# Attention and MLP in one kernel: products with values in three uneven blocks a pair of heads, and four other pieces of work issued later

## The chip, the cores and the metric

The kernel runs on one core of a Trainium2 chip. The metric is the device time of one execution in microseconds (us); lower is better. The engines are named as in the profile: PE is TensorE (matrix products), PEld its loading of weights, DVE VectorE, ACT ScalarE, POOL GpSimd, and SP SyncE, which here issues every DMA.

## The reference, cut to what matters

```python
xn = layernorm(x)                                   # x: 2048 x 640
q, k, v = split(xn @ wqkv)                          # 32 heads of 20
scores = where(0 <= i - j < 256, q @ k.T * 20**-0.5, -1e9)
s = (softmax(scores) @ v) @ wo
h = relu(xn @ w1 + b1) ** 2                         # 1536 wide
g = silu(h @ w2 + b2)
return x + s * g
```

All inputs are float32. A row of scores sees itself and 255 rows before it, so a tile of 128 rows needs three tiles of keys.

## The kernel before, in words

**Precision.** Every product of projections and of the MLP is made three times, from a high part (rounded by an ACT copy) and a low part (the rest, a subtraction on DVE or POOL) of each operand: high x high, high x low, low x high. Weights come as raw tiles by DMA (`piece`, three raw buffers), ACT makes the high part, and `subtract` (line 758) puts the low parts off: each is queued with `later(0.9 + 0.7 * k, go)` (line 771).

**First stage, to about 116 us.** x is normalized, transposed and split; the values v, and the first group of q and k are made and stored to DRAM; the normalized x goes to DRAM too (`xs_d`).

**The scan, to about 775 us.** It goes over 16 pairs of heads with 16 steps each. Step s makes the scores of one tile of queries for both heads (`scores`, tile sps), whose row maxima DVE takes (`maxima`; `max_rows` transposes four steps' maxima at a time, and small DMAs put them beside q as extra rows, `qs<-mrow`). Nine steps later (LAG) the transposed scores of one tile of keys are made (`scores_t`, tile stps, one buffer), ACT takes the exponential into a tile p (`exps`, eight buffers), and POOL masks two corners. Another two steps later (PLAG, line 45) the tile p is due for the products with the values. These are made in blocks: at each fourth step `values(p, g)` (line 533) multiplies the four tiles p of steps 4g to 4g + 3 into one PSUM bank `ot` of four columns of 128 queries. A head's values are only 21 wide (20 and a column of ones, which gives the sum of the row), so a product uses a strip of 32 columns of PE, and four strips work side by side. Then `evac` copies two finished columns to SBUF (`osb`) with ACT and stores them to `o_d[g]`, one DRAM tensor for each quarter of the queries.

**Fillers.** Between these products the planner puts the other products of the kernel (the remaining groups of q and k, then the MLP). They run in two halves of 64 rows that work side by side. The order of all instructions is written out by this Python code as it runs: a clock of its own (`clock`) advances by a price for each product (`COST`, line 42, and PV = 1.57 for a block of values), `pace` (line 1199) is the price of everything divided by the steps, and `fill(upto)` (line 1201) takes filler products until the clock has reached a time. In each step the scores come first, then fillers to 0.4 of the step (line 1257), then, where due, the block of values, else fillers to the step's end (lines 1262 to 1266). `later(wait, fn)` issues something when this clock has gone on by `wait`.

**DMAs.** All go through SP in the written order. Large loads wait in `bulk`, and `issue` (line 683), called twice a step with 0.9, starts them against a credit: each has a price (`load_xb`, line 853: ten loads of 256 KB of the normalized x at 0.4 each; loads of q and k at 0.7).

**The MLP** goes over eight blocks (two halves of its width, each over four blocks of 512 rows): first products into `hps` (relu and square), then into `yps` in eight groups (four row tiles by two halves of 320 columns), whose sums `ysb` DVE adds to b2 or to the first half's (`yin`, loaded from DRAM).

**The end.** When a quarter of the queries has all its pairs, `invert` (line 1055) loads its row sums, takes the reciprocal on DVE and stores it. `load(u)` (line 1098) loads an eighth of the attention's result with these reciprocals, `turn_out` multiplies and splits it, and the output stage (`out_filler`, from about 783 us) multiplies it with wo, with g and adds x. In the last block of the MLP `late()` (line 913) calls the first such loads at the start of its fourth and fifth group of products.

Of the kernel before, what the change touches and what calls it, by code (L numbers as in the profile page):

```python
# [15 lines left out]
P = 128  # L16
# [5 lines left out]
NT = S // P  # L22
# [18 lines left out]
WARM2 = 10  # L41
COST = {P: 0.067, 2 * P: 0.12, HALF: 0.147, 3 * P: 0.172, BT: 0.23}
SCALE = DH ** -0.5
PV = 1.57
PLAG = 2
NEG = -1.0e30
EPS = 1e-5
SETTLE = 0.45
# [5 lines left out]
def f32(ap):  # L54
    return ap.bitcast(F32)
# [3 lines left out]
def attn_mlp_kernel(ctx: ExitStack, tc, x, wqkv, wo, w1, b1, w2, b2, out):  # L59
# [470 lines left out]

    ot = po_.tile([P, 4, P], F32, tag="o", name="ops")

    def values(p, g):
        for kb in range(4 * g, 4 * g + 4):
            pt = pts.pop((p, kb))
            ts = range(kb, min(kb + 3, NT))
            same, other = [t for t in ts if t % 2 == kb % 2], [t for t in ts if t % 2 != kb % 2]
            parts = [same] if kb % 8 < 6 else [[t] for t in same]
            for part in parts + [other]:
                for hh in range(2):  # L540
                    if not part:
                        continue
                    t = part[0]
                    r0 = 32 * (2 * hh + t % 2)
                    c0 = t // 2 % 4
                    first = t % 8 < 2 and kb == max(0, t - 2) or kb == 0
                    nc.tensor.matmul(ot[r0:r0 + VW, c0:c0 + len(part), :], vps[p][:, kb // 4, kb % 4, hh, :], pt[:, hh, :].rearrange("p (t n) -> p t n", n=P)[:, t - kb:part[-1] - kb + 1:2, :], start=first, stop=part[0] == kb, skip_group_check=True)  # L547
        clock[:2] = [max(clock[:2]) + PV] * 2

        def evac():  # L550
            osb = at2.tile([P, 2, P], F32, tag="osb", name="osb")
            nc.scalar.activation(osb, ot[:, 2 * g % 4:2 * g % 4 + 2, :], AF.Copy)
            post(o_d[g][p], osb.rearrange("p e n -> p (e n)"), 0.8)
        later(SOON, evac)


# [201 lines left out]
    def subtract(tag, jobs):  # L758
        left = [len(jobs)]

        def put_off(k, job):
            def go():
                if item in lows:
                    lows.remove(item)
                    job()
                    left[0] -= 1
                    if not left[0]:
                        held[0] -= 1
            item = (tag, go)
            lows.append(item)  # L770
            later(0.9 + 0.7 * k, go)
        for k, job in enumerate(jobs):
            put_off(k, job)

# [78 lines left out]
    def load_xb(b):  # L853
        xb = [bigp.tile([P, KC * BT], F32R, tag="big", name=f"xb{p}_{b}") for p in range(2)]
        cs = [slice(c * BT, (c + 1) * BT) for c in range(KC)]
        its = [bulk_dma(0.4, f32(xb[p])[:, c], xs_d[p][b][:, c]) for p in range(2) for c in cs]
        return xb, its

    def filler():
# [53 lines left out]
        def late():  # L913
            j = lates[0]
            lates[0] += 1
            if j >= 3:
                load(0)
            if j >= 4:
                load(1)
            if j >= 6:  # L920
                turn_out(0, 0)
            if j >= 7:
                turn_out(0, 1)
                load(2)

        for n, (hf, b) in enumerate(blocks):
# [13 lines left out]
            def used(n=n, b=b, nxt=nxt):  # L940
                if n == NB - 1:
                    shut.discard("11")
                if n == last:
                    shut.discard("o")
                if n < last and blocks[n + 1][1] != b:
                    nxt.extend(load_xb(blocks[n + 1][1]))
            parts = [(th, fp) for th in range(2) for fp in range(WIDE // 2, NFH // 2)]
            parts[len(parts) // 2:len(parts) // 2] = range(WIDE)
            for m, u in enumerate(parts):
# [95 lines left out]
        return 4 * (u // 2) + u % 2 + 2 * t2  # L1045

    def stored(g):
        return NP * NT - NT + 4 * g + 3 + LAG + PLAG

    rec_d = [dram.tile([2, H, MT], F32, name=f"rec_{g}") for g in range(NB)]  # L1050
    recs = {}

    lates = [0]

    def invert():
        for g in range(NB):
            over = state[2] >= 10 ** 6
            if not over and state[2] < stored(g) + 3:
                return
            if g not in recs:  # L1060
                rows = o_d[g].rearrange("p (h r) n -> (p h) r n", h=2)
                recs[g] = at2.tile([P, P], F32, tag="rec", name="rec")
                for par in range(2):
                    nc.sync.dma_start(recs[g][64 * par:64 * (par + 1)], rows[:, 32 * par + DH].rearrange("h (j n) -> h j n", n=P))
            elif recs[g] is not None and (state[2] >= stored(g) + 5 if not over else True):
                nc.vector.reciprocal(recs[g], recs[g])
                nc.sync.dma_start(rec_d[g].rearrange("a h (j n) -> (a h j) n", n=P), recs[g])
                recs[g] = None

    def room_of(tag, name):  # L1070
        if tag == "p32":
# [124 lines left out]

    fl = filler()
    steps = NP * NT + LAG + PLAG
    pace = (8 * (KC - 1) * 15 * COST[BT] + 2 * NB * (15 * (WIDE * COST[BT] + 2 * (NFH - WIDE) * COST[MT]) + 8 * 18 * COST[HALF]) + NP * (2 * NT * COST[3 * P] + NB * PV)) / (steps - 1)

    def fill(upto):
        soon()
# [10 lines left out]
    with tc.manual_schedule(engines={E_.PE, E_.Activation, E_.DVE, E_.Pool, E_.SP}):  # L1213
# [7 lines left out]
        for s in range(steps):  # L1221
            state[2] = s
            vload[0] = 0.2 * (s % 4 == 0) + 0.5 * (s % 4 == 3)
            post_all()
            invert()
            if s >= NP * NT - NT + LAG + 2:
                fetch_y()
            issue(RATE)
            a, b, e = (at_step(s - lag) for lag in (0, LAG, LAG + PLAG))
            if a:  # L1230
                p, q = a
                if q == 0:
                    ensure_bulk(loads)
                if s == 2:
                    ones_rows(1)
                if q == 2 and p < NP - 1:
                    assert made_for(p + 1, 0)
                    loads = [bulk_dma(0.7, *l) for l in pair_loads(p + 1, 0)]
                if q == LAG and p < NP - 1:
                    assert made_for(p + 1, 1)  # L1240
                    loads += [bulk_dma(0.7, *l) for l in pair_loads(p + 1, 1)]
                if q == LAG + 4 and p < NP - 1:
                    load_v(p + 1)
            rows = None
            if a:
                sc = scores(p, q)
            if b:
                stp = scores_t(*b)
            if s % 4 == 0 and 0 < s <= NP * NT:
                rows = max_rows((s - 1) // NT, (s - 1) % NT // 4, stp[0] if b else pair_tile())  # L1250
            if a:
                maxima(*a, *sc)
            if b:
                exps(*b, *stp)
            if rows:
                rows()
            fill((s + EARLY_FILL) * pace)
            post_all()
            issue(RATE)
            flush()  # L1260
            tick()
            if e and e[1] % 4 == 3:
                fill((s + 1) * pace - PV)
                values(e[0], e[1] // 4)
            else:
                fill((s + 1) * pace)
        finish()
# [30 lines left out]
```

## Time and profile before

| | us |
|---|---|
| median of three runs | 859.34 (858.82 to 859.89) |
| the profiled execution's own time | 859.53 |
| its span, first to last instruction | 857.8 |
| last block of values starts | 774.7 |
| first output product starts | 782.9 |

The profile is that of one execution. Busy time is summed by engine; a row of a group has the line, the engine, the operation, output and inputs, how often it ran, busy time and the mean of one, and the idle time of the engine before it. A row of the timeline has the start, the time to the end of the group of like instructions (counted with x), the engine and the line, and in brackets how long the engine stood idle before, and for whom. In the table by windows each engine's busy time stands with its number of instructions, then PE's clock (1.00 is full speed), the DMA share and GB/s. A row of waits has the total, the number and the longest.

### The profile page before, as it was taken

To read this page: it belongs to the slowest core of one execution; us is meant where nothing else is said; L and a number is where in the kernel's file an instruction comes from. 1 tells how busy PE (TensorE), PEld (TensorE's weight loads), DVE (VectorE), ACT (ScalarE), POOL (GpSimd) and SP (SyncE) were. 2 spreads that over 40 slices of the span, in tenths; PEclk is the share of its full clock that TensorE was granted. 3 is DMA by queue.
4 is the path that set the end of the run, shared out by engine and by line. 5 is a ranking of instruction groups with operands and counts; after the bars stand their busy time and mean duration, and the time that the engine had idled before them with its cause. 6 is when DMAs were issued, how large, how long until landed. Compare 5 with 4: busy or idle time off the path is not lost.

```text
span 857.8 us, 25542 instructions
## 1 busy us (share of the span) xinstructions
PE 845.3 (99%) x10160; PEld 786.1 (92%) x10160; DVE 459.1 (54%) x1370; ACT 421.6 (49%) x792; POOL 328.7 (38%) x652
## 2 busy tenths in 40 slices
PE   9999999999999999999999999999999989999998
PEld 8999999888888899999999989999999989999997
DVE  7652136656577545455445466655445444435764
ACT  5222114545556753754654764854754743753321
POOL 6010002334333553553543543643543533541443
PEclk9999999999999999999999999999999999999999
DMA  7997587869889564355266245585376274367992
GB/s 250 327 399 279 170 206 267 263 210 286 278 260 275 146 215 130 84 172 151 77 198 184 61 130 162 144 256 165 77 208 191 61 229 127 126 155 198 277 258 111
DMA packets 94366, 166.42 MB, mean 194 GB/s; under 512 B 10920, under 2 KB 43816, under 8 KB 93224
## 3 DMA queue, kind: packets, MB, share of 16 engines
q1 hardware_dynamic: 94248, 164.80, 63.3%
q8 instruction: 80, 1.31, 0.6%
q14 instruction: 38, 0.31, 0.1%
HBM read 93.66 MB, written 70.52 MB: 191 GB/s over the span
## 4 chain that ended last, share of the span: by engine, by line
PE 93%; DMA 2%; DVE 2%; ACT 1%; issue 1%; SPq 1%; POOL 0%; DVEq 0%
PE hps L469 20%; PE yps L469 20%; PE qkps L469 13%; PE ops L547 10%; PE wops L607 8%; PE vps L229 8%; PE stps L519 5%; PE sps L479 4%; PE qkps L206 3%; PE tps L173 1%; DMA qs<-mrow 1%; DMA qs<-q_d 1%; DMA yin<-y 1%; DVE junk L487 0%; DMA xt<-in_A_x_dram 0%
## 5 line engine op out<-in xcount | busy, mean ns | idle before, releaser
L487 DVE CUSTOM_DVE_ANT_0 junk<-sps,mask 128x384 bf16<-128x384 f32 (+2 forms) x512 | 272.6, 532 | 251.7 <-PE hps L469 70.1
L525 ACT ACTIVATE p<-stps 128x768 f32<-128x768 f32 (+2 forms) x256 | 197.5, 772 | 264.6 <-PE stps L519 216.2
L526 POOL TENSOR_SCALAR_AFFINE_SELECT p<-p 128x256 f32<-128x256 f32 x256 | 107.7, 421 | 332.7 <-ACT p L525 327.8
L469 PE MATMUL yps<-w,hh 64*128 64x320 f32 x1536 | 229.2, 311 | 1.8 <-DVE ysb L996 1.7
L469 PE MATMUL hps<-xb,w 64*128 64x256 f32 (+1 forms) x2100 | 218.6, 305 | 0.0
L469 PEld LDWEIGHTS hps<-xb,w 64*128 64x128 f32 x2100 | 199.2, 187 | 6.2 <-issue 5.1
L469 PEld LDWEIGHTS yps<-w,hh 64*128 64x128 f32 x1536 | 182.2, 186 | 7.5 <-issue 3.4
L469 PE MATMUL yps<-w,hl 64*128 64x320 f32 x768 | 173.5, 310 | 0.0
L479 PE MATMUL sps<-ks,qs 60*128 60x384 f32 (+2 forms) x512 | 141.5, 341 | 1.3 <-DVE mt L487 1.1
L519 PE MATMUL stps<-qs,ks 62*128 62x384 f32 (+2 forms) x512 | 134.5, 332 | 2.4 <-DMA qs<-mrow 2.4
L469 PEld LDWEIGHTS yps<-w,hl 64*128 64x128 f32 x768 | 113.5, 186 | 1.8 <-issue 1.7
L469 PE MATMUL qkps<-xT,wgkh 64*128 64x512 f32 x320 | 100.6, 395 | 0.0
L469 PE MATMUL qkps<-xT,wgqh 64*128 64x512 f32 x320 | 98.1, 392 | 0.0
L528 POOL TENSOR_SCALAR_AFFINE_SELECT p<-p 128x256 f32<-128x256 f32 x224 | 94.1, 420 | 0.0
L547 PE MATMUL ops<-p,vp 128*21 128x128 f32 (+1 forms) x2112 | 92.8, 313 | 0.0
L519 PEld LDWEIGHTS stps<-qs,ks 62*128 62x128 f32 x512 | 87.1, 188 | 3.4 <-issue 2.7
L479 PEld LDWEIGHTS sps<-ks,qs 60*128 60x128 f32 x512 | 85.3, 185 | 4.2 <-DVE mt L487 2.7
L547 PEld LDWEIGHTS ops<-p,vp 128*21 128x21 f32 x2112 | 65.2, 100 | 23.6 <-issue 11.4
L229 PE MATMUL vps<-wv,xT 128*128 128x320 f32 x480 | 71.5, 308 | 0.0
L229 PEld LDWEIGHTS vps<-wv,xT 128*128 128x128 f32 x480 | 70.5, 188 | 0.1
L966 POOL TENSOR_TENSOR hl<-sq,hh 128x512 fp32r<-128x512 f32 x48 | 62.2, 1296 | 19.0 <-ACT sq L965 18.8
L607 PE MATMUL wops<-wo,oT 128*128 128x320 f32 x384 | 61.6, 309 | 0.7 <-DVE ysb L996 0.7
(104 smaller groups left out, 1166.8 us busy)
## 6 DMA issues: line engine op xcount, KB each, us to landing
ks<-k_d SPq DMA_DIRECT2D x64, 240.0 KB
qs<-q_d SPq DMA_DIRECT2D x64, 240.0 KB
xb<-xs SPq DMA_DIRECT2D x60, 256.0 KB
xs<-xT SPq DMA_DIRECT2D x8, 1280.0 KB
k_d<-shm SPq DMA_DIRECT2D x19, 512.0 KB
q_d<-shm SPq DMA_DIRECT2D x19, 512.0 KB
y<-ysb SPq DMA_DIRECT2D x28, 320.0 KB
o<-osb SPq DMA_DIRECT2D x64, 128.0 KB
```

Source lines behind the costliest of these rows:

```text
L206: nc.tensor.matmul(ps, wt[:, c, :], xT[part][b][:, c * BT + t0:c * BT + t0 + n], start=m == 1, stop=m == 3 * KC)
L229: nc.tensor.matmul(ps, xT[xp][b][:, c * BT + t * P: c * BT + (t + 1) * P], wv[wp][:, c, nh * HALF:(nh + 1) * HALF], start=first and m == 0 ...
L469: return nc.tensor.matmul(out, a[r], b_[r], skip_group_check=True, **kw)
L479: nc.tensor.matmul(ss[hh][:, :nk], qs[i][o, q * P:(q + 1) * P], ks[i][o, k0 * P:k0 * P + nk], start=True, stop=True)
L487: nc.vector.tensor_tensor_reduce(out=junk[:, :nk], in0=ss[hh][:, :nk], in1=mask[:, 3 * P - nk:], scale=1.0, scalar=-3.0e38, op0=ALU.add, o ...
L519: nc.tensor.matmul(tps[:, hh, :n], ks[i][o, kb * P:(kb + 1) * P], qs[i][o, kb * P:kb * P + n], start=True, stop=True)
L525: nc.scalar.activation(p32[:, :, :n], tps[:, :, :n], AF.Exp, scale=SCALE)
L526: nc.gpsimd.affine_select(p32[:, :, 0:P], p32[:, :, 0:P], pattern=[[0, 2], [1, P]], compare_op=ALU.is_ge, fill=0.0, base=0, channel_multip ...
L528: nc.gpsimd.affine_select(p32[:, :, 2 * P:], p32[:, :, 2 * P:], pattern=[[0, 2], [-1, P]], compare_op=ALU.is_gt, fill=0.0, base=0, channel ...
L547: nc.tensor.matmul(ot[r0:r0 + VW, c0:c0 + len(part), :], vps[p][:, kb // 4, kb % 4, hh, :], pt[:, hh, :].rearrange("p (t n) -> p t n", n=P ...
L607: nc.tensor.matmul(ps, a, b_, start=j == 0, stop=j == n - 1)
L966: nc.gpsimd.tensor_sub(hh[1][:, :BT], sq, f32(hh[0]))
```

## The change

Five edits go together. The products with values of a pair of heads come in three blocks, of steps 0 to 5, 6 to 11 and 12 to 15 (`CUTS`), in place of four of four steps, each with its own price for the planner (`PVS`), and they are due one step after the exponential in place of two (`PLAG`). The copy of a block's result is of three columns, in one or two instructions, and its stores are cut where the quarter changes; they are posted without the wait of 0.8. Low parts of weights are put off by 1.0 more. Loads of x are issued 1.0 later and at a price of 0.6. In the MLP's last block the first load of the attention's result moves from the fourth group to the fifth. The inversions follow the new blocks: each quarter is stored at another step, is loaded two steps (in place of three) after that and inverted at four (in place of five), only one may be under way at a time, with one buffer, and after the scan a count of calls keeps a load and its inversion apart.

```diff
--- before.py
+++ after.py
@@ -41,8 +41,9 @@
 WARM2 = 10
 COST = {P: 0.067, 2 * P: 0.12, HALF: 0.147, 3 * P: 0.172, BT: 0.23}
 SCALE = DH ** -0.5
-PV = 1.57
-PLAG = 2
+CUTS = (0, 6, 12, NT)
+PVS = (2.25, 2.25, 1.42)
+PLAG = 1
 NEG = -1.0e30
 EPS = 1e-5
 SETTLE = 0.45
@@ -530,8 +531,9 @@
 
     ot = po_.tile([P, 4, P], F32, tag="o", name="ops")
 
-    def values(p, g):
-        for kb in range(4 * g, 4 * g + 4):
+    def values(p, i):
+        lo, hi = CUTS[i], CUTS[i + 1]
+        for kb in range(lo, hi):
             pt = pts.pop((p, kb))
             ts = range(kb, min(kb + 3, NT))
             same, other = [t for t in ts if t % 2 == kb % 2], [t for t in ts if t % 2 != kb % 2]
@@ -545,12 +547,19 @@
                     c0 = t // 2 % 4
                     first = t % 8 < 2 and kb == max(0, t - 2) or kb == 0
                     nc.tensor.matmul(ot[r0:r0 + VW, c0:c0 + len(part), :], vps[p][:, kb // 4, kb % 4, hh, :], pt[:, hh, :].rearrange("p (t n) -> p t n", n=P)[:, t - kb:part[-1] - kb + 1:2, :], start=first, stop=part[0] == kb, skip_group_check=True)
-        clock[:2] = [max(clock[:2]) + PV] * 2
+        clock[:2] = [max(clock[:2]) + PVS[i]] * 2
 
         def evac():
-            osb = at2.tile([P, 2, P], F32, tag="osb", name="osb")
-            nc.scalar.activation(osb, ot[:, 2 * g % 4:2 * g % 4 + 2, :], AF.Copy)
-            post(o_d[g][p], osb.rearrange("p e n -> p (e n)"), 0.8)
+            c0, c1 = lo // 2, hi // 2
+            osb = at2.tile([P, 3, P], F32, tag="osb", name="osb")
+            c = c0
+            while c < c1:
+                n = min(4 - c % 4, c1 - c)
+                nc.scalar.activation(osb[:, c - c0:c - c0 + n], ot[:, c % 4:c % 4 + n, :], AF.Copy)
+                c += n
+            for g in range(c0 // 2, (c1 + 1) // 2):
+                d0, d1 = max(c0, 2 * g), min(c1, 2 * g + 2)
+                post(o_d[g][p, :, (d0 - 2 * g) * P:(d1 - 2 * g) * P], osb[:, d0 - c0:d1 - c0].rearrange("p e n -> p (e n)"))
         later(SOON, evac)
 
 
@@ -768,7 +777,7 @@
                         held[0] -= 1
             item = (tag, go)
             lows.append(item)
-            later(0.9 + 0.7 * k, go)
+            later(1.9 + 0.7 * k, go)
         for k, job in enumerate(jobs):
             put_off(k, job)
 
@@ -853,7 +862,7 @@
     def load_xb(b):
         xb = [bigp.tile([P, KC * BT], F32R, tag="big", name=f"xb{p}_{b}") for p in range(2)]
         cs = [slice(c * BT, (c + 1) * BT) for c in range(KC)]
-        its = [bulk_dma(0.4, f32(xb[p])[:, c], xs_d[p][b][:, c]) for p in range(2) for c in cs]
+        its = [bulk_dma(0.6, f32(xb[p])[:, c], xs_d[p][b][:, c]) for p in range(2) for c in cs]
         return xb, its
 
     def filler():
@@ -913,9 +922,8 @@
         def late():
             j = lates[0]
             lates[0] += 1
-            if j >= 3:
+            if j >= 4:
                 load(0)
-            if j >= 4:
                 load(1)
             if j >= 6:
                 turn_out(0, 0)
@@ -943,7 +951,7 @@
                 if n == last:
                     shut.discard("o")
                 if n < last and blocks[n + 1][1] != b:
-                    nxt.extend(load_xb(blocks[n + 1][1]))
+                    later(1.0, lambda: nxt.extend(load_xb(blocks[n + 1][1])))
             parts = [(th, fp) for th in range(2) for fp in range(WIDE // 2, NFH // 2)]
             parts[len(parts) // 2:len(parts) // 2] = range(WIDE)
             for m, u in enumerate(parts):
@@ -1045,27 +1053,35 @@
         return 4 * (u // 2) + u % 2 + 2 * t2
 
     def stored(g):
-        return NP * NT - NT + 4 * g + 3 + LAG + PLAG
+        return NP * NT - NT + min(c for c in CUTS if c >= 4 * (g + 1)) - 1 + LAG + PLAG
 
     rec_d = [dram.tile([2, H, MT], F32, name=f"rec_{g}") for g in range(NB)]
     recs = {}
 
     lates = [0]
+    calls, ready = [0], [0]
 
     def invert():
+        calls[0] += state[2] >= 10 ** 6
         for g in range(NB):
             over = state[2] >= 10 ** 6
-            if not over and state[2] < stored(g) + 3:
+            if over and calls[0] < ready[0]:
+                return
+            if not over and state[2] < stored(g) + 2 or over and calls[0] < ready[0]:
                 return
             if g not in recs:
+                if any(r is not None for r in recs.values()):
+                    return
+                ready[0] = calls[0] + 3
                 rows = o_d[g].rearrange("p (h r) n -> (p h) r n", h=2)
-                recs[g] = at2.tile([P, P], F32, tag="rec", name="rec")
+                recs[g] = at2.tile([P, P], F32, tag="rec", bufs=1, name="rec")
                 for par in range(2):
                     nc.sync.dma_start(recs[g][64 * par:64 * (par + 1)], rows[:, 32 * par + DH].rearrange("h (j n) -> h j n", n=P))
-            elif recs[g] is not None and (state[2] >= stored(g) + 5 if not over else True):
+            elif recs[g] is not None and (state[2] >= stored(g) + 4 if not over else True):
                 nc.vector.reciprocal(recs[g], recs[g])
                 nc.sync.dma_start(rec_d[g].rearrange("a h (j n) -> (a h j) n", n=P), recs[g])
                 recs[g] = None
+                ready[0] = calls[0] + 2
 
     def room_of(tag, name):
         if tag == "p32":
@@ -1196,7 +1212,7 @@
 
     fl = filler()
     steps = NP * NT + LAG + PLAG
-    pace = (8 * (KC - 1) * 15 * COST[BT] + 2 * NB * (15 * (WIDE * COST[BT] + 2 * (NFH - WIDE) * COST[MT]) + 8 * 18 * COST[HALF]) + NP * (2 * NT * COST[3 * P] + NB * PV)) / (steps - 1)
+    pace = (8 * (KC - 1) * 15 * COST[BT] + 2 * NB * (15 * (WIDE * COST[BT] + 2 * (NFH - WIDE) * COST[MT]) + 8 * 18 * COST[HALF]) + NP * (2 * NT * COST[3 * P] + sum(PVS))) / (steps - 1)
 
     def fill(upto):
         soon()
@@ -1259,9 +1275,10 @@
             issue(RATE)
             flush()
             tick()
-            if e and e[1] % 4 == 3:
-                fill((s + 1) * pace - PV)
-                values(e[0], e[1] // 4)
+            if e and e[1] + 1 in CUTS:
+                i = CUTS.index(e[1] + 1) - 1
+                fill((s + 1) * pace - PVS[i])
+                values(e[0], i)
             else:
                 fill((s + 1) * pace)
         finish()
```

## The prediction, made before the changed kernel was run

> **What bounds the kernel now.** I read the page's busy shares first, then the table by stage, then the chain of waits, and last the timeline around single blocks and stalls.
>
> ```profile
> span 857.8 us, 25542 instructions
> PE 845.3 (99%) x10160; PEld 786.1 (92%) x10160; DVE 459.1 (54%) x1370; ACT 421.6 (49%) x792; POOL 328.7 (38%) x652
> PE 93%; DMA 2%; DVE 2%; ACT 1%; issue 1%; SPq 1%; POOL 0%; DVEq 0%
> 524.00:746.00 222.00, 219.52 (x3169) 204.59 (x3165) 114.35 (x396) 125.09 (x240) 102.20 (x211) 0.99 0.55 158
> 782.80:857.80 75.00, 70.63 (x480) 70.40 (x480) 46.35 (x64) 19.13 (x28) 31.09 (x30) 0.99 0.74 212
> ```
>
> PE is busy 99% of the span, and the last stage (output products, from 782.8) runs almost without a gap until 853.5. In the long stage shown (524 to 746) PE lacks 2.5 us in 222, and one stall makes nearly all of that. So only two things can move the time: what PE's own work costs, switches between kinds of products included, and a handful of stalls. DVE at 54% and ACT at 49% do not bound as averages, but they decide when a score bank comes free.
>
> **The blocks of values, fixed cost.** One pair of heads has 66 products with values, seen as 132 records. They run in four column strips; all others around them run in two halves of 64 rows.
>
> ```profile
> L547 PE MATMUL ops<-p,vp 128*21 128x128 f32 x1344 | 88.6, 274 | 0.0
> L547 PE MATMUL ops<-p,vp 128*21 128x256 f32 x768 | 75.1, 382 | 0.0
> 161.30:171.70 10.40, 1.52 (x40) 1.14 (x40) 0.00 (x0) 0.38 (x1) 1.00 0.90 266
> 180.90:190.50 9.60, 1.28 (x28) 0.90 (x28) 0.00 (x0) 0.38 (x1) 1.00 0.67 211
> ```
>
> 128 more columns cost 382 - 274 = 108 ns a record, 0.216 us a product of two records. In a strip the longest queue of the block of steps 12 to 15 is five such units, 1.08 us; of steps 4 to 7 six, 1.30 us. The table by windows shows 1.28 and 1.52 busy, so about 0.21 us of a block does not depend on its length.
>
> ```profile
> 319.43 0.45 PE L469 MATMUL yps<-w,hh 64*128 64x320 f32 x3
> 319.81 1.52 PE L547 MATMUL ops<-p,vp 128*21 128x256 f32 x40
> 321.25 0.41 PE L469 MATMUL yps<-w,hl 64*128 64x320 f32 x1
> 321.26 0.44 PE L479 MATMUL sps<-ks,qs 60*128 60x384 f32 x1
> 321.51 0.31 PE L469 MATMUL yps<-w,hh 64*128 64x320 f32 x1
> 321.54 0.34 PE L519 MATMUL stps<-qs,ks 62*128 62x384 f32 x1
> ```
>
> Three costs belong to one block. Ahead of it: the last of the three yps products (0.31 each) starts at 319.57, the block at 319.81; of these 0.24 us the product needs the 0.147 that line 42 books for it, so 0.09 are lost. Inside: the block begins at 319.81 and the next product at 321.25, 1.44 us for 1.30 of columns, 0.14 lost. Behind it: the two restarting products take 0.41 and 0.44 where their like take 0.31 and 0.34, 0.10 lost. Sum 0.33 us a block. The change makes 3 blocks of 4 in each of 16 pairs, with the same products: 16 x 0.33 = **5.3 us less**. Bounds: 16 x 0.14 = 2.2 if only the part inside goes, and 16 x 0.36 = 5.8 by the planner's own prices (4 x 1.57 = 6.28 against 2.25 + 2.25 + 1.42 = 5.92). I take 5.3, the sum of what the rows show.
>
> [...]
>
> **The blocks of values, what becomes late.** A step is booked at 638.7/266 = 2.40 us (line 1199), after the change at 632.9/265 = 2.39. Fillers run to 0.4 of it, 0.96, then comes the block. Booked at 2.25 it ends at 3.21, 0.82 into the next step, which so has 1.57 us left until the next pair of scores; before, 0.96 + 1.57 = 2.53 left 2.27. After a block of four steps (1.42) nothing is short. So in 32 of the 256 steps the engines that empty the banks have about 1.6 us.
>
> ```profile
> 301.90 0.34 PE L519 MATMUL stps<-qs,ks 62*128 62x384 f32 x1
> 303.74 0.41 POOL L528 TENSOR_SCALAR_AFFINE_SELECT p<-p 128x256 f32<-128x256 f32 x1
> 303.98 0.33 PE L479 MATMUL sps<-ks,qs 60*128 60x384 f32 x1
> 304.15 0.33 PE L519 MATMUL stps<-qs,ks 62*128 62x384 f32 x1
> 305.55 0.25 ACT L500 ACTIVATE row<-stps 8x128 f32<-8x128 f32 x1
> 306.49 0.33 PE L479 MATMUL sps<-ks,qs 60*128 60x384 f32 x1
> 306.72 0.34 PE L479 MATMUL sps<-ks,qs 60*128 60x384 f32 x1
> 308.14 0.08 DVE L487 DVE_READ_ACCUMULATOR2_ANT mt<- 128x1 f32 x1
> L888 DVE TENSOR_TENSOR slo<-qkps,shm 128x512 fp32r<-128x512 f32 x32 | 22.0, 687 | 6.6 <-ACT shm L885 6.6
> ```
>
> DVE's second maximum is out at 308.22, 1.73 us after the step's first score product (306.49); the second score product of the next step, which reuses that bank, comes 0.23 after its first. With 1.6 us between steps it is asked for at 1.83: 0.10 to spare where DVE has nothing else, and a wait of 0.4 to 0.6 where a subtraction (0.69 in the row of slo, the low parts some less) stands ahead. The first block ends so in step 6 of a pair; the second (steps 6 to 11) ends in the next pair's row 0, whose maxima are only 128 wide. There the bank of stps decides: its row of maxima is read until 305.80, 1.65 after 304.15, a wait of about 0.05. Behind a waiting score product the whole of PE queues, and POOL, ACT and DVE with it. I take 0.06 us on average over 32 steps, **2.0 us more**; bounds nothing (all fits) and 0.4 each, 12.8 us (a subtraction ahead every time).
>
> The lag before values falls from two steps to one. The trace has no such wait; from the stps product to POOL's second mask it is 301.90 to 304.15, 2.25 us. The block begins one step (2.4) and some 0.8 of fillers after that product, and reaches the last step's p in its last sixth, another 1.6 later: 4.8, about 2.6 us to spare, cost nothing. If ACT and POOL fell behind by more, PE would stand in the block. The p buffers (8) are reused two steps after their block in place of three, behind products that PE has by then done: nothing. ACT copies stay 64 (one of three columns, two, one a pair); stores of values go from 64 to 80, 16 more issues on SP, one for each pair: nothing. They are issued 0.8 earlier, so SP waits for ACT's copy with later DMAs behind it; the row's DMA is issued ahead of that copy: nothing, unless ACT is late by microseconds.
>
> **Stalls that the other edits touch.**
>
> ```profile
> 289.10 0.44 PE L479 MATMUL sps<-ks,qs 60*128 60x384 f32 x1 [0.69 <-DVE mt L487]
> 502.34 1.01 DVE L799 TENSOR_TENSOR w<-raw,w 128x384 fp32r<-128x384 f32 x1 [2.22 <-ACT w L796]
> 503.80 0.41 PE L469 MATMUL yps<-w,hh 64*128 64x320 f32 x1 [1.13 <-DVE ysb L996]
> DVE w L799 <- ACT w L796: 12.4, 13, 2.2
> 519.41 1.23 DVE L799 TENSOR_TENSOR w<-raw,w 128x384 fp32r<-128x384 f32 x2
> 524.18 0.28 PE L469 MATMUL hps<-xb,w 64*128 64x256 f32 x1
> xb<-xs SPq DMA_DIRECT2D x60, 256.0 KB
> 690.09 5.29 SPq L693 DMA_DIRECT2D xb<-xs  x10
> 699.36 1.19 SPq L504 DMA_DIRECT2D qs<-mrow  x2
> 706.17 0.44 PE L519 MATMUL stps<-qs,ks 62*128 62x384 f32 x2 [2.43 <-DMA qs<-mrow]
> 758.93 1.90 SPq L1107 DMA_DIRECT2D ob<-o  x4
> 761.56 1.16 SPq L1064 DMA_DIRECT2D rec<-o  x2
> 766.22 0.95 DVE L1066 RECIPROCAL rec<-rec 128x128 f32<-128x128 f32 x1 [2.83 <-DMA rec<-o]
> 768.30 0.41 PE L469 MATMUL yps<-w,hh 64*128 64x320 f32 x1 [0.58 <-DVE ysb L996]
> 782.86 1.40 PE L607 MATMUL wops<-wo,oT 128*128 128x320 f32 x8 [0.68 <-DVE ysb L996]
> ```
>
> *Low parts.* DVE stands at the subtraction until ACT has the high part: 12.4 us in 13 waits. Two of them held the maxima or ysb up until PE stopped, 0.69 and 1.13, 1.8 us. A microsecond more in the plan covers all but the longest waits (2.2). But work of another order deals new hands, so I take **1.0 us less**, bounds 1.8 less and 1.0 more. The raw buffers are held 1 us longer: the last subtraction of w1's second half ends at 520.64 and the first product that reads it starts at 524.18, so 1 us more, or 2 with two pieces in turn, does not bind.
>
> *Loads of x.* Ten loads of 256 KB were issued in 5.29 us from 690.09; the rows of maxima issued at 699.36 came so late that PE stood 2.43 and went on at 706.17. At a price of 0.6 for 0.4 the credit of 0.9 issues 1.5 in place of 2.25 at a time, 384 KB for 576, and they begin 1 us later. This happened once in six such loads (60 issues by ten). I take it gone, **2.4 less**, bounds 2.4 less and 2.4 more (it strikes another load). The products that need this x come after the block's whole second product (lines 982 to 1031): no cost.
>
> *End.* Both loads of values' first quarter now go out at the fifth group, ten issues of about 0.48 (1.90 for four) in a row, 4.8 us on SP, with yin's load behind; the second inversion is read two steps later, the later ones one after another. The two stalls there (0.58 and 0.68) may go or grow: I take **nothing**, bounds 1.3 less and 2.5 more. The load of unit 2 moves into the output stage, ahead of the products of unit 1: nothing.
>
> **Sum.** The profiled execution took 859.53 (0.2 above the median of 859.34). 859.53 - 5.3 + 2.0 - 1.0 - 2.4 = **852.8 us**. [...]
>
> **Rivals.** (1) *Stalls only move*: the blocks give 3.3 net, the four stalls come back elsewhere; 859.5 - 3.3 = 856.2. For it: of 13 DVE waits only two reached PE, which is chance. (2) *The fixed cost isn't PE's to save*: only 0.14 a block goes, and the stall behind x comes back elsewhere; 859.5 - 2.2 + 2.0 - 1.0 = 858.3, no change. Against it: the three parts are seen at both edges. (3) *The short step outruns DVE*, slower: in the step after each block of six, PE's second score product stands until DVE has the bank free. What the forecast gains is 5.3 + 3.4 = 8.7 us; over 32 steps the break-even is 0.27 a step. With a subtraction ahead every time, 0.4, it is 12.8: 859.5 - 8.7 + 12.8 = 863.6. For it: a margin of 0.10 only; against it: DVE is busy 54%, and row 0's maxima are short. (4) *The end pays*: yin behind ten issues, 852.8 + 2.5 = 855.3.
>
> **How the numbers follow.** Forecast 0.51 (849.5 to 855), rival 1 0.15, rival 2 0.08, rival 3 0.21, rival 4 0.05. The range 849.0 to 862.0 holds all but half of rival 3 and the case that short steps cost nothing and the end gains (859.5 - 5.8 - 4.2 - 1.3 = 848.2). A measurement of this kernel can tell 0.2%, 1.7 us: faster 0.71, same 0.08, slower 0.21.
>
> **What would show it.** Right: 48 blocks with fixed cost as before, no wait of PE on qs<-mrow, subtractions that start without a wait on ACT. Wrong: PE rows of sps with a wait on DVE's maxima, or of stps on ACT's row, some 0.3 each in the steps after blocks of six; values that wait for POOL; PE stalls at the end on ysb behind yin.

## The result: 870.96 us against 859.62, and the profile after

The changed kernel takes **870.96 us** (median of four, 870.36 to 871.34); the kernel before, run beside it, 859.62. The ratio is 1.0128, 95% interval 1.0111 to 1.0146: slower by 1.3%, where 852.8 was forecast and 862.0 was the upper end of the range.

The page of the changed kernel: span, busy time by engine, and PE's share of the chain that ended last.

```profile
span 869.2 us, 25572 instructions
PE 848.2 (98%) x10160; PEld 793.8 (91%) x10160; DVE 457.4 (53%) x1370; ACT 420.5 (48%) x792; POOL 329.7 (38%) x652
PE 9%; DMA 2%; DVE 1%; SPq 0%; issue 0%; DVEq 0%
```

The chain of before covered the whole span, 93% of it PE. Here it could be followed back from the end only to 760.3 us, so the shares add up to 12% and can't be set against those of before; what it covers, though, is the stretch that matters. The table by windows says where the time goes. Its columns are the stretch and its length, busy time of PE, PEld, DVE, ACT and POOL with the number of instructions, PE's granted clock, the DMA share and GB/s.

```profile
116.00:781.40 665.40, 658.71 (x8933) 609.55 (x8932) 359.84 (x1186) 370.64 (x698) 281.15 (x592) 1.00 0.58 175
781.40:796.70 15.30, 15.29 (x104) 15.30 (x105) 5.48 (x9) 2.74 (x4) 3.50 (x4) 1.00 0.91 218
796.70:817.00 20.30, 12.76 (x51) 12.23 (x50) 10.82 (x14) 5.30 (x8) 5.51 (x5) 0.67 0.99 229
817.00:869.20 52.20, 48.21 (x328) 47.95 (x327) 29.31 (x42) 11.11 (x17) 21.50 (x21) 0.99 0.65 185
```

The first output product starts at 781.41, 1.45 us earlier than before (782.86). From there to the end of the last one before took 70.63 us; now the same 480 products end at 865.21, after 83.80. **The output stage is 13.2 us longer, and that is more than the whole loss**: -1.45 + 13.2 - 0.3 behind the last product = 11.4, the difference of the spans. It happens in 20 us: from 796.7 to 817.0 PE is busy for 12.76 and its clock is at 0.67. The chain of waits through this place, in order of time (start, length, what):

```profile
781.41 4.65 PE wops L616 x30
...
787.39 11.07 DMA ob<-o
...
798.47 0.02 SPq L1112
...
798.97 6.81 DMA rec<-rec
...
807.09 3.58 DMA yk<-y
...
810.69 0.13 DVE rec L1081
```

And the timeline of SP, DVE and PE around it, in order of time:

```profile
775.19 1.37 SPq L1079 DMA_DIRECT2D rec<-o  x2
779.23 0.33 SPq L1082 DMA_DIRECT2D rec<-rec  x1
782.96 2.30 SPq L1112 DMA_DIRECT2D xres<-in_A_x_dram  x5
785.83 2.27 SPq L1123 DMA_DIRECT2D ob<-o  x4
785.83 0.95 DVE L1081 RECIPROCAL rec<-rec 128x128 f32<-128x128 f32 x1
798.67 1.56 DVE L1139 TENSOR_TENSOR ob<-ob,sums 128x512 f32<-128x512 f32 x2 [7.70 <-DMA ob<-o]
798.97 0.38 SPq L1082 DMA_DIRECT2D rec<-rec  x1
800.69 3.57 PE L616 MATMUL wops<-wo,oT 128*128 128x320 f32 x12 [3.65 <-DVE res L1203]
805.85 1.20 SPq L1079 DMA_DIRECT2D rec<-o  x2
810.69 0.95 DVE L1081 RECIPROCAL rec<-rec 128x128 f32<-128x128 f32 x1 [7.51 <-DMA yk<-y]
812.04 3.30 PE L616 MATMUL wops<-wo,oT 128*128 128x320 f32 x11 [3.89 <-DVE res L1203]
```

Two delays, one behind the other. **First**, the second quarter's row sums are loaded at 775.19 and its reciprocals stored at 779.23. The kernel before, for comparison (the load stands in the prediction, at 761.56):

```profile
769.89 0.34 SPq L1067 DMA_DIRECT2D rec<-rec  x1
775.43 1.99 SPq L1107 DMA_DIRECT2D ob<-o  x4
778.63 2.29 SPq L1096 DMA_DIRECT2D xres<-in_A_x_dram  x5
785.83 1.20 SPq L1064 DMA_DIRECT2D rec<-o  x2
```

There they were stored at 769.89, so that unit 2 (`ob<-o`, the first unit of the second quarter) was loaded at 775.43, ahead of the five loads of x. Now it stands behind them, at 785.83. DVE has its multiplication next in line and stands 7.70 us. Behind it in DVE's order are the sums that empty PE's banks (`res`, line 1203), so PE stands 3.65. **Second**, the reciprocals of the third quarter have one buffer. DVE has made them by 786.78, but their store goes out at 798.97: SP has waits of its own ahead of it, the last of them, by the chain, until unit 2's load has landed at 798.46. So the first delay is one of the things that make the second. The store takes 6.81 us to land; only then can SP load the fourth quarter's row sums, at 805.85 (before: 785.83). DVE has that reciprocal next, stands 7.51 us (the row names `yk<-y`, a load issued right behind the row sums, but the reciprocal reads only these), and PE stands again, 3.89. After each stall PE's products come at half speed (the twelve behind the first stall take 3.57 us; eleven at full clock, from 794.83, took 1.77). The stalls beyond the usual spacing are 7.9 us; the other 5.3 of the 13.2 are, as what is left, the half clock. Full DMA engines alone (0.91 and 0.99 here) don't explain it: in the kernel before they were as full from 797 to 812 (1.07), and PE ran on.

The rest of the change in the waits (engine and line, whom it waits for, total, times, longest):

```profile
PE wops L616 <- DVE res L1203: 7.5, 2, 3.9
PEld sps L480 <- DVE mt L488: 3.2, 11, 0.4
PE stps L520 <- DMA qs<-mrow: 3.1, 2, 2.0
DVE w L808 <- ACT w L805: 0.6, 1, 0.6
```

DVE's waits for ACT's high part fell from 12.4 us in 13 to 0.6 in one. The wait for rows of maxima did not go.

### The profile page after: what moved, and what is told of

Its sections match the earlier page's. It is cut to its first block, busy times and chain, and to the rows that moved or that the text cites. A ratio compares the mean times of both kernels' runs of the same rounds, so it can differ in the third digit from the quotient of the medians.

```text
span 869.2 us, 25572 instructions
## 1 busy us (share of the span) xinstructions
PE 848.2 (98%) x10160; PEld 793.8 (91%) x10160; DVE 457.4 (53%) x1370; ACT 420.5 (48%) x792; POOL 329.7 (38%) x652
## 5 line engine op out<-in xcount | busy, mean ns | idle before, releaser
L470 PE MATMUL hps<-xb,w 64*128 64x256 f32 (+1 forms) x2100 | 213.3, 305 | 0.0
L470 PEld LDWEIGHTS hps<-xb,w 64*128 64x128 f32 x2100 | 194.9, 187 | 5.1 <-issue 3.8
L470 PE MATMUL yps<-w,hl 64*128 64x320 f32 x768 | 178.2, 309 | 0.0
L480 PE MATMUL sps<-ks,qs 60*128 60x384 f32 (+2 forms) x512 | 134.5, 339 | 0.4
L520 PE MATMUL stps<-qs,ks 62*128 62x384 f32 (+2 forms) x512 | 127.3, 337 | 4.2 <-DMA qs<-mrow 3.1
L470 PEld LDWEIGHTS yps<-w,hl 64*128 64x128 f32 x768 | 119.2, 185 | 0.9 <-issue 0.9
L480 PEld LDWEIGHTS sps<-ks,qs 60*128 60x128 f32 x512 | 80.8, 185 | 5.0 <-DVE mt L488 3.2
L520 PEld LDWEIGHTS stps<-qs,ks 62*128 62x128 f32 x512 | 79.7, 187 | 5.8 <-issue 3.6
L616 PE MATMUL wops<-wo,oT 128*128 128x320 f32 x384 | 66.2, 325 | 8.2 <-DVE res L1203 7.5
L616 PEld LDWEIGHTS wops<-wo,oT 128*128 128x128 f32 x384 | 61.9, 201 | 9.0 <-DVE res L1203 8.1
```

The lines of the kernel that those rows point to most:

```text
L470: return nc.tensor.matmul(out, a[r], b_[r], skip_group_check=True, **kw)
L480: nc.tensor.matmul(ss[hh][:, :nk], qs[i][o, q * P:(q + 1) * P], ks[i][o, k0 * P:k0 * P + nk], start=True, stop=True)
L520: nc.tensor.matmul(tps[:, hh, :n], ks[i][o, kb * P:(kb + 1) * P], qs[i][o, kb * P:kb * P + n], start=True, stop=True)
L616: nc.tensor.matmul(ps, a, b_, start=j == 0, stop=j == n - 1)
```

## The experiments

All are timed beside the kernel before. "First output" is the start of the first output product, "output stage" from there to the end of the last.

| run | first output | output stage | median us | ratio (95%) |
|---|---|---|---|---|
| before | 782.86 | 70.63 | 859.62 | |
| the change | 781.41 | 83.80 | 870.96 | 1.0128 (1.0111 to 1.0146) |
| e1 blocks alone | 780.24 | 77.75 | 863.04 | 1.0031 (1.0016 to 1.0047) |
| e2 all but the blocks | 779.14 | 72.88 | 857.94 | 0.9972 (0.9957 to 0.9987) |
| e3 two inversions at a time | 788.22 | 75.43 | 863.54 | 1.0051 (1.0029 to 1.0072) |
| e4 unit 2 first | 780.62 | 82.62 | 869.49 | 1.0104 (1.0079 to 1.0130) |
| e5 both | 782.55 | 76.69 | 865.36 | 1.0059 (1.0038 to 1.0080) |
| e6 both, block early | 783.56 | 72.93 | 860.52 | 1.0000 (0.9977 to 1.0023) |
| e7 blocks of two | 805.52 | 71.06 | 882.93 | 1.0250 (1.0233 to 1.0266) |
| e8 low parts and x alone | 775.79 | 70.63 | 853.10 | 0.9907 (0.9893 to 0.9922) |
| e9 inversions alone | 783.12 | 75.05 | 864.20 | 1.0063 (1.0041 to 1.0085) |
| e10 old inversions | 781.87 | 74.80 | 861.98 | 1.0029 (1.0005 to 1.0052) |
| e11 old inversions, block early | 773.06 | 75.57 | 855.01 | 0.9941 (0.9920 to 0.9962) |
| e12 four, six, six | 776.17 | 72.16 | 854.33 | 0.9930 (0.9903 to 0.9956) |
| e13 last pair in fours | 779.76 | 70.63 | 858.43 | 0.9981 (0.9971 to 0.9991) |
| e14 e11, last pair in fours | 773.60 | 70.63 | **850.70** | 0.9890 (0.9874 to 0.9907) |

The two columns of times are of the one profiled execution. For e3 it was the longest of its ten (869.77), so its first output is late; for e13 the shortest of its twelve (856.53).

**The theory** was: the blocks save what was forecast in the scan, and the end loses it and more, because the block of steps 6 to 11 finishes the second quarter too late and the inversions go one at a time. **The rival**: the short step behind a block of six, or the fixed cost that isn't PE's, makes the blocks slow by themselves.

**e1, the blocks alone**, and **e2, all but the blocks.**

```diff
--- before.py (e1: CUTS, PVS, PLAG, values, evac, stored, pace as in the change, and)
-                recs[g] = at2.tile([P, P], F32, tag="rec", name="rec")
+                recs[g] = at2.tile([P, P], F32, tag="rec", bufs=1, name="rec") if g % 2 == 0 else at2.tile([P, 3, P], F32, tag="osb", name="rec")[:, 0, :]
--- after.py (e2)
-CUTS = (0, 6, 12, NT)
-PVS = (2.25, 2.25, 1.42)
-PLAG = 1
+CUTS = (0, 4, 8, 12, NT)
+PVS = (1.57, 1.57, 1.57, 1.57)
+PLAG = 2
```

> The kernel before with the new blocks of values (six, six and four steps, one step later, their copies and stores) and nothing else; the inversions keep their spacing of three and five steps, but count from the new blocks, so the second quarter's sums are loaded at step 264 and inverted after the scan. Theory A (the loss sits in the output stage: unit 2 is loaded behind five loads of x, and one buffer for inversions holds DVE up): the scan ends 2 to 5 us earlier than before, unit 2 is still late, there is no second stall; 859 to 864 us. Theory B (the long blocks cost more in the scan than their switches save): the first output product starts no earlier than before (782.9) and the time is over 865 us.

> The kernel after with four blocks of four steps again, two steps late, at the old price: only the loads of x, the low parts and the inversions are later. Theory A: the second quarter is inverted at step 262, in time for unit 2 ahead of the loads of x, so the first stall of the output stage is gone; the inversions one at a time may leave part of the second; 855 to 863 us. Theory B: about the time of before, 857 to 861.

The blocks alone cost 0.31% though their first output comes 2.6 us earlier: the output stage is 7.1 longer. Theory A said no second stall; there are two, of 1.2 us at 797 and 2.4 at 818. The other four edits gain 0.28%. Neither makes 1.28%; the two together do. e1 also shows the price of the short step where nothing is done for it, in its waits:

```profile
DVE w L808 <- ACT w L805: 10.0, 11, 1.7
PEld sps L480 <- DVE mt L488: 8.0, 22, 0.6
PE sps L480 <- DVE mt L488: 1.7, 7, 0.4
```

PE itself waits 1.7 us for the maxima and its weight loads 8.0, against 1.1 and 2.7 in the same two rows of before (seven waits). In the whole change only the weight loads wait, 3.2 us in 11: with the low parts later no subtraction stands ahead of the maxima. (e10 below, which is e1 with the later low parts and loads of x, has the same 3.2.)

**e3, two inversions at a time; e4, unit 2 loaded first; e5, both.**

```diff
--- after.py (e3 and e5: the waits of one inversion for the other are out, two buffers as in e1; e4 and e5: the load)
-                if any(r is not None for r in recs.values()):
-                    return
-                ready[0] = calls[0] + 3
...
     def out_filler(wo_part):
+        load(2)
         while len(xts) < 4:
```

> The kernel after, but inversions may run two at a time again (a second buffer, no count of calls). Theory A: the stall of 3.9 us at 808 in the output stage and the clock's drop behind it go, the one at 797 stays: 863 to 867 us. Theory B: no difference, 870 to 872.

> The kernel after, but unit 2 of the attention's result is loaded ahead of the five loads of x at the start of the output stage. Theory A: the stall of 3.7 us at 797 and the clock's drop behind it go, the one at 808 stays, 863 to 867 us. Theory B: no difference, 870 to 872.

> The kernel after with both mends of the output stage: two inversions at a time and unit 2 loaded ahead of the loads of x. Theory A (two delays at the end, each hidden behind the other when only one is mended): the output stage takes 71 to 74 us from its first product, against 83.8, and the time is 857 to 861 us. Theory B (unit 2 has nothing to do with it, the one buffer is all): as with two inversions alone, 862 to 865.

e3 took the time expected, but not with the stalls expected: its profiled execution has neither of the two, only 1.2 us at 823 and 1.5 at 834. e4 did not come out as expected: the first stall went, and the second took its place, at twice the length.

```profile
808.74 0.95 DVE L1081 RECIPROCAL rec<-rec 128x128 f32<-128x128 f32 x1 [11.20 <-DMA rec<-o]
810.10 3.57 PE L616 MATMUL wops<-wo,oT 128*128 128x320 f32 x12 [7.89 <-DVE res L1204]
```

DVE gets the fourth quarter's row sums at 808.74, only 2 us earlier than in the changed kernel, because the third quarter's store still goes out at 796.87 only; PE merely came there sooner. The first delay had been covered by the second, so its removal was worth 0.24 points, within the intervals nothing, and not the 4 us and the half clock that it had in the timeline. e5 missed too (865.36, a stall of 3.1 left at 792.8, ahead of which DVE stands 6.05 for a reciprocal): unit 2 first brought nothing on top of two inversions either (863.54 without it), and the two together are not enough.

**e6, the block of six right after the scores of its step** (on top of e5).

```diff
-            fill((s + EARLY_FILL) * pace)
+            early = 0.05 if e and e[1] + 1 in CUTS and PVS[CUTS.index(e[1] + 1) - 1] > 2 else EARLY_FILL
+            fill((s + early) * pace)
```

> As both ends mended, and in a step with a block of six the block starts right after the scores, not at 0.4 of the step, so that it ends within its own step. Theory: the step after a block is 2.2 us and not 1.6, DVE has the bank free in time and the waits of PE in steps 6 and 0 go, 2 to 3 us less than with both ends alone. Rival: those waits are hidden by other delays, the same within 1 us.

The waits for the maxima (all but 0.3 us) and those for rows of maxima are gone, as meant, and the time is 4.8 us less than e5's, where 2 to 3 were expected. But a new stall of 5.5 us stands at the end of the MLP, and with it the half clock (the first product behind it takes 0.63 us where its like take 0.31, and the run's mean clock is 0.988); the ten runs spread from 856.5 to 863.7.

```profile
772.50 0.63 PE L470 MATMUL yps<-w,hh 64*128 64x320 f32 x1 [5.48 <-DVE ysb L1004]
```

**e7, blocks of two steps** (on top of e2): eight blocks a pair for four, 64 more in all, with the same products.

```diff
-CUTS = (0, 4, 8, 12, NT)
-PVS = (1.57, 1.57, 1.57, 1.57)
+CUTS = tuple(range(0, NT + 1, 2))
+PVS = (0.96,) * 8
```

> The kernel of the other edits alone (four-step blocks), but with eight blocks of two steps a pair at 0.96 each: 64 more blocks of the same products. It measures the fixed cost of a block. By the rows of before, 0.33 us a block: 21 us more than the 857.9 of the other edits alone, 877 to 881. If only the part inside a block counts (0.14), 9 us more, 866 to 868.

25.0 us more than e2, 0.39 a block; by the two ratios, 0.0278 of 860, it is 0.37. That is above the 877 to 881 expected; the forecast had 0.33, read from the edges of one block. The fixed cost of a block is real, and PE pays it: it is busy 868.7 us for e2's 844.1.

**e8, low parts and loads of x alone; e9, the inversions alone** (each on the kernel before, with those lines of the change).

> The kernel before with only two edits: low parts 1.0 later, loads of x 1.0 later and at 0.6. By the prediction's step 3.4 us less (the stalls at 288, 502 and 703 go), 855.5 to 857. If stalls only move, 858.5 to 861. Beside the other edits alone (857.9), which has these two and the late inversions, it prices the inversions: its output stage stays at 70.6 us against 72.9.

> The kernel before with only the later inversions (two and four steps, one at a time with one buffer and a count of calls) and the first load of the result at the fifth group. By the difference of the two runs before it (other edits 857.9, low parts and loads of x alone 853.1) they cost 4.8 us: 863 to 866 us, some 3 ahead of the output stage and 2 in it. If the late inversions hurt only together with the new blocks: 859 to 861.

e8 is 853.10: more than the forecast's 3.4 us for these two. Its first output comes 7.1 earlier. The stalls in the scan fell from 7.2 to 2.7 us in sum (counted from the start of one product to the next where that is over 0.36 us, less 0.25 for the product; PE's idle time alone fell from 5.5 to 1.9), and with the one at 703 went 3.4 us of half clock (e8's mean clock is 0.999 over 850.7 us, at most 2.6 us at half). e9 is 864.20: the inversions cost 0.63%, some 4 to 5 us, without any block changed, nearly all in the output stage (75.05 for 70.63, with a stall of 2.5 at 800; the run's mean clock is 0.996 over 862.4 us, some 7 us at half, where the kernel before has 4.3).

**e10, the change with the old inversions; e11, with the block early too; e12, with blocks of four, six and six.**

```diff
--- after.py (e10: invert() and late() as before, two buffers as in e1)
--- e11: e10 and the edit of e6
--- e12: e11 and
-CUTS = (0, 6, 12, NT)
-PVS = (2.25, 2.25, 1.42)
+CUTS = (0, 4, 10, NT)
+PVS = (1.57, 2.25, 2.06)
```

> The kernel after with the inversions and the first load as before (three and five steps, two at a time, fourth group); blocks of six, loads of x and low parts stay. Theory: unit 2 still comes behind the loads of x, since its quarter is now finished by the second block, so the output stage takes 75 to 78 us as with the blocks alone, and the scan keeps its three stalls behind the rows of maxima: 862 to 866 us. Rival, the edit of the inversions is the whole loss: 853 to 857.

> As the one before, and blocks of six start right after the scores of their step. Theory: the waits after blocks and the stalls behind the rows of maxima go (they came with the shortened steps), 5 to 9 us less: 854 to 859 us, what is left being the end. Rival: the stalls behind the rows come from the queue of loads and stay: 860 to 863.

> As the one before, with blocks of four, six and six steps, so that the second quarter is finished at step 259 and unit 2 is loaded ahead of the loads of x. If the blocks' switches are worth 0.33 to 0.4 us each where nothing is late behind them, this beats low parts and loads of x alone (853.1): 846 to 851 us. If the end or the step after a block still costs, 852 to 858.

e10 takes 9 us back, e11 another 7.0. e12 missed the better of its two cases: 854.33, no better than e8, though its scan is 3.5 us shorter than e8's once the stalls are taken off (769.6 against 773.1; 2.5 by idle time alone). It finishes the second quarter with step 9 and the third with step 15, later than before, and has stalls of 2.5 and 1.6 behind `ysb` at 762 and 768; ahead of the first, DVE stands 7.1 us for row sums. That pointed to the one thing that e1 to e12 had all left in place wherever there were blocks of six.

**e13 and e14, the last pair of heads in blocks of four**, all other pairs in six, six and four.

```diff
+def cuts(p):
+    return ((0, 4, 8, 12, NT), (1.57,) * 4) if p == NP - 1 else (CUTS, PVS)
...
-        lo, hi = CUTS[i], CUTS[i + 1]
+        lo, hi = cuts(p)[0][i:i + 2]
```

> The changed kernel, but the last pair of heads alone gets its products with values in four blocks of four steps again, so that the second quarter of the queries is finished by a block that ends in step 7 of that pair and not in step 11. If the late second quarter is what holds up unit 2's load at the end: the second unit is ready before the five loads of x, the stall of 3.96 us goes and the half clock behind it, the output stage takes 75 to 79 us (what the inversions one at a time leave) and the time is 862 to 866 us. If the inversions alone make the end, or one delay takes the other's place as where unit 2 was loaded first: the output stage stays at 82 to 84 us and the time at 868 to 872.

> The kernel with blocks of six right after the scores and the old inversions (855.01), with the last pair in four blocks of four steps. If the blocks' gain in the scan was given back because two quarters of the last pair are finished late: the output stage goes from 75.6 to 70.6 to 72 us and the time to 849 to 852 us, below the 853.1 of the later low parts and loads of x alone. If the end's stalls have another cause (rows finished late are not what DVE waits for): 854 to 857.

e13, which is the changed kernel but for the last of its 16 pairs, takes 858.43. **Two blocks of six in one pair had cost 12.5 us.** Its timeline of SP and its output stage by windows:

```profile
753.65 1.20 SPq L1085 DMA_DIRECT2D rec<-o  x2
763.74 0.33 SPq L1088 DMA_DIRECT2D rec<-rec  x1
773.86 1.97 SPq L1129 DMA_DIRECT2D ob<-o  x4
777.82 2.46 SPq L1118 DMA_DIRECT2D xres<-in_A_x_dram  x5
784.67 1.70 SPq L1085 DMA_DIRECT2D rec<-o  x2
```
```profile
779.70:854.30 74.60, 70.63 (x480) 70.40 (x480) 46.24 (x63) 19.14 (x28) 31.23 (x30) 1.00 0.80 223
```

The second quarter is inverted 15 us earlier, unit 2 goes ahead of x again, the fourth quarter's row sums come at 784.67, and PE runs through the output stage in 70.63 at full clock, with one inversion at a time and one buffer. I had expected 75 to 79, from e9, and 862 to 866 us; so one inversion at a time need not cost anything, though it did in e9 (75.05) and e2 (72.88), without any longer block. What makes that difference is not settled. What e13 still pays is one stall, at the end of the MLP: DVE stands 5.04 for reciprocals (`rec<-rec`), and PE 4.36 behind it, with half clock from there (the next product takes 0.63; the run's mean clock is 0.998 over 854.4 us, some 3.4 us at half). In time e13 is no faster than e2 (857.94), which has blocks of four in all pairs: the ratios are 0.9981 and 0.9972, with intervals that overlap.

e14 takes that away as well (old inversions, block early) and is the fastest of all, **850.70**, ratio 0.9890 (0.9874 to 0.9907), within the 849 to 852 expected.

```profile
span 848.5 us, 25560 instructions
PE 838.6 (99%) x10160; PEld 788.7 (93%) x10160; DVE 458.8 (54%) x1370; ACT 422.9 (50%) x792; POOL 330.1 (39%) x652
PE 96%; ACT 1%; DVE 1%; DMA 1%; issue 1%; SPq 0%; DVEq 0%
```

PE is busy 838.6 us for the 845.3 of before, in 32 - 2 = 30 blocks of six and 19 of four, 49 for 64. Not all of that is the blocks: e8, with 64 blocks, is at 841.5, so they and their early place make 2.9.

## Why the prediction was wrong, step by step

**The step that failed is "End".** It priced the end at nothing, bounds 1.3 less and 2.5 more, and said of unit 2 that its load "moves into the output stage, ahead of the products of unit 1: nothing". Measured: 13.2 us. The forecast asked whether the data would be there before PE needs them. It didn't ask what stands behind the waiting instruction. DVE took its work in written order, and between the multiplication for unit 2 and the next one stand the sums that empty PE's banks: one of them, for products that PE had done by 793, ran at 800.15 only, behind the multiplication (798.67). SP took its own in written order too: unit 2's load (785.83) stood behind five loads of x (782.96), the fourth quarter's row sums (805.85) behind a store (798.97) that itself stood 12 us after its reciprocal. It had also read "one after another" for the inversions, and gave it no price. The rival of the right place (4, the end pays) had 2.5 us, one late load, and not two in a row with half clock behind each. e13 shows the cause by taking only the last pair's blocks away (and with them the later steps at which its quarters are inverted); e9 and e10 show that the inversions add to it. Either alone makes the output stage 4 to 7 us longer (the blocks 77.75 in e1 and 74.80 in e10, the inversions 75.05 in e9), the two together 13.2.

**The blocks' fixed cost, 5.3 less: right by e7, though no run takes it out of the change by itself.** e7 gives 0.37 to 0.39 a block for the forecast's 0.33. In the changed kernel:

```profile
312.02 2.15 PE L549 MATMUL ops<-p,vp 128*21 128x256 f32 x48
314.10 0.41 PE L470 MATMUL yps<-w,hl 64*128 64x320 f32 x1
314.10 0.33 PE L480 MATMUL sps<-ks,qs 60*128 60x128 f32 x1
...
326.70 2.17 PE L549 MATMUL ops<-p,vp 128*21 128x128 f32 x56
328.79 0.41 PE L470 MATMUL yps<-w,hh 64*128 64x320 f32 x1
328.80 0.44 PE L480 MATMUL sps<-ks,qs 60*128 60x384 f32 x1
...
330.43 0.34 PE L480 MATMUL sps<-ks,qs 60*128 60x384 f32 x1
```

The restarting products take 0.41 and 0.44, as behind a block of four: the same edge, three times a pair for four.

**The short step, 2.0 more: about right, with a slip.** The pair of scores at 328.80 is followed by the next at 330.43, 1.63 later (1.57 to 1.6 was forecast), and the waits are small (0.4 at most). The forecast had the two blocks the wrong way round: the block of steps 0 to 5 ends before row 0 of the next pair (the 128 wide scores at 314.10), that of 6 to 11 in step 6. The sum is the same. Blocks and short steps together: with the stalls taken off, counted as for e8, the first output product comes at 773.3 for 775.7 before, 2.4 less (1.9 by idle time alone); forecast 3.3 less. For fifteen pairs PE's busy time says much the same: 841.5 in e13 for 844.1 in e2. Rival 3 needed a subtraction ahead of the maxima; e1 has it (8.0 us of waits of the weight loads) and the change doesn't, because its low parts are later. That link the forecast did not see.

**Low parts, 1.0 less: right in the mechanism.** 12.4 us of waits became 0.6. With the loads of x, and without the blocks, it is worth the 0.93% of e8.

**Loads of x, 2.4 less: wrong in the change.** The stall at 703 to 706 is still there.

```profile
693.91 0.90 SPq L702 DMA_DIRECT2D xb<-xs  x2
695.33 0.98 SPq L702 DMA_DIRECT2D xb<-xs  x2
...
699.63 0.62 SPq L702 DMA_DIRECT2D qs<-q_d  x1
700.85 1.14 SPq L505 DMA_DIRECT2D qs<-mrow  x2
```
```profile
707.36 0.45 PE L520 MATMUL stps<-qs,ks 62*128 62x384 f32 x2 [1.98 <-DMA qs<-mrow]
708.81 3.37 PE L549 MATMUL ops<-p,vp 128*21 128x256 f32 x48
```

The rows of maxima are now issued behind the last four loads of x and four of q and k of 240 KB, and PE goes on 6.5 us after their issue, where it was 6.8 before. Behind the stall the block of 48 records takes 3.37 us where it takes 2.15: half clock again (0.50 from 707.9 to 711.3). The stalls in the scan sum to 8.2 us for 7.2, so for the stalls rival 1 ("only move") held. Why they fall at these places in one order of instructions and not in another (none in e1, none with the block early) is not settled; each edit deals the whole order anew.

So the forecast's 852.8 was within reach, but mostly by the low parts and loads of x: e8 alone is at 853.1. e14 is at 850.7; that the blocks of fifteen pairs and their early place add 2.4 us to e8's gain (1.5 by the ratios) is not shown, as the intervals of the two overlap. The change as made lost 12.5 us at one pair of sixteen.

## What to carry to other kernels

When a block is made longer, ask what its last one finishes: here the same edit saved some 2 to 3 us of PE's time in fifteen pairs, and cost 12.5 in the sixteenth, where the next stage waits for the result. Price a late load not by the gap until PE needs it but by everything queued behind the instruction that waits for it, on its engine and on the queue that issues it. And where two delays follow one another, mending the first alone shows nothing; mend what makes both late.

## What the runs showed of the hardware

In the traces of the two kernels PE's clock is at 1.00 or at 0.50, and the half clock comes in pieces of 3.41 us or twice that: one of 3.41 from 706.6 in the kernel before; one of 3.41 from 707.9 and two of 6.83, from 800.1 and 810.3, in the changed one. In both another begins behind the last product, at 856.8 and 868.4, and lasts to the end of the span. Within each of the two runs all of them start on one grid of that period: 92.2, 102.4 and 160.4 us behind the first in the changed kernel (27, 30 and 47 periods), 150.2 in the kernel before (44). Two other runs show more of it in their mean clock: 0.92 over 83.4 us of e4's output stage, some 13 us at half, and 0.988 over e6's 860.8 us, some 21. A PE stall of some 2 to 4 us was thus dearer than it looks: 7.9 us of stalls brought 5.3 more. The length of the stall doesn't decide it: behind one of 1.98 us in the changed kernel (it ends at 707.36) a piece began at 707.9, while e1, whose longest was 2.4, has a mean clock of 0.999 over 862.2 us, at most 2.6 us at half and so no whole piece. Nor did it end when PE was busy again: from 800.69 to 806.80 in the changed kernel PE was busy for all of the 6.11 us, with its clock at 0.50 throughout.
